# A gated attention and MLP decode step: one 128-row weight transfer cut into 102 and 26 rows

## The chip, the cores and the metric

The kernel runs on one core of a Trainium2 chip. The metric is the device time of one execution in microseconds (us), and the time of a kernel is the median of its runs. The profile used here records one execution: when each instruction of each engine ran, when each DMA packet moved, and when each DMA engine reported its share of a transfer done.

## The reference, cut to what matters

One token for each of 4 sequences passes through cached attention (32 heads of 128, a cache of 8192 positions) and through a gated MLP, and a sigmoid gate mixes the two.

```python
q = (x @ wq)                                  # [4, 32 heads, 1, 128]
p = softmax(einsum("bhqd,bhkd->bhqk", q, k_cache) * Dh ** -0.5)
o = einsum("bhqk,bhkd->bhqd", p, v_cache)     # [4, 32, 1, 128]
a = o.reshape(4, 1, 4096) @ wo                # wo: [4096, 1024]
y = ((silu(x @ w_gate) * (x @ w_up)) @ w_down) * sigmoid(x @ w_r)
b = x + y
g = sigmoid((x * gate_w).sum(-1))
return g * a + (1 - g) * b                    # [4, 1, 1024]
```

All inputs are bf16. The two caches are 268 MB each, and with the weights some 576 MB are read once.

## The kernel before

**A ring of SBUF and one queue.** All large inputs pass through one SBUF tile, `ring`, and every load into it is issued from SyncE's DMA queue in a hand-written order: wq, the gate, K and V of four heads at a time (`k_pair`, `v_pair`, 128 rows of 64 KB), w_up, w_down, the last V, and at the end wo. TensorE multiplies with the loaded data as the moving operand; VectorE turns K in 32x32 blocks.

**The tail.** wo is 4096 x 1024. `wov` views it as 8 blocks `g`, in each of which partition `p` holds 4 rows (slots `r` = 0 to 3, 2 KB each); a block is 1 MB. Blocks 0 and 1, and 2 and 3, come by one transfer each (`wo_two`); blocks 4, 5 and 6 by one each (`wo_block`, line 439). The last block, 7, comes in pieces so that TensorE can follow it closely: slots 0 and 1 in one transfer (512 KB), slot 2 in one (256 KB, 128 rows of 2 KB), and slot 3 in two halves of 512 columns (128 KB each, line 442). The list `cuts` holds these pieces:

```python
    cuts = [(g, 0, FR) for g in range(4, NWB - 1)] + [(NWB - 1, 0, 2), (NWB - 1, 2, 3)] + [(NWB - 1, FR - 1, FR, n) for n in range(NH)]
    last += [wo_block(*cut) for cut in cuts]
```

`wo_block` issues the load at once and returns `use`, which is called later and adds the block's products to two PSUM accumulators, `acc(0)` and `acc(1)`, one for each half of the 1024 output columns: per slot one matmul of 128 x 4 by 128 x 512 for each half (line 296, in `mm_acc`). The first half of slot 3 completes `acc(0)`, the second half completes `acc(1)`.

**The end.** VectorE copies `acc(0)` to SBUF (line 694) and SyncE's queue stores it (line 695); ScalarE copies `acc(1)` (line 696) and its own queue stores it (line 697).

**Semaphores of the transfers.** The transfers from SyncE take eight completion semaphores in turn. Before a transfer is issued on a semaphore, SyncE waits until the transfer that used it eight places earlier has landed, where nothing else implies that already.

**Engines of a transfer.** One transfer is divided by rows over DMA engines of the core (16 in all). Each engine works off its rows, one descriptor per row, then writes its completion (a packet of 4 bytes) and goes to its share of the next transfer in the queue. A transfer counts as landed when all of its engines have reported. Three early transfers are narrower than 128 rows: x (4 rows), two vectors of one row each, and, beside w_down, two transfers of 12 rows of 10 KB (line 411) and one of 8 rows of 2 KB (line 412).

Of the kernel before, what the change touches and what calls it, by code (L numbers as in the profile page):

```python
# [112 lines left out]
def kernel(  # L113
# [15 lines left out]
    nc = tc.nc  # L129
    P = 128  # L130
    Bn, Sq, D = A_x.shape
# [17 lines left out]
    FR = 4  # L149
    FG = F // (P * FR)  # L150
    NB = 512
    NH = D // NB
# [86 lines left out]
    n = 1  # L239
# [19 lines left out]
    for half in range(2):  # L259
        for e in range(2):  # L260
            nc.gpsimd.tensor_copy(out=R[:, 2 * half + e].rearrange("p (n j) -> p n j", n=4),
                                  in_=ident[:, 64 * half + e:64 * half + 64:2].unsqueeze(1).to_broadcast([P, 4, 32]))
# [21 lines left out]
    LT = const.tile([P, FR, H // FR, Bn], BF)  # L284
# [7 lines left out]
    def acc(n):  # L292
        return A_ps[n][32 * n:32 * n + Bn]

    def mm_acc(n, lhsT, rhs, start=False):
        nc.tensor.matmul(acc(n), lhsT=lhsT, rhs=rhs, start=start, stop=True, skip_group_check=True)  # L296
# [36 lines left out]
    wov = A_wo.rearrange("(g p r) n -> p g r n", p=P, r=FR)  # L333
# [86 lines left out]
    NWB = H // WB  # L420
# [8 lines left out]
                                 rhs=OT[:, WB * g0 + k:WB * g1:WB, :], start=True, stop=True, skip_group_check=True)  # L429
        nc.vector.tensor_copy(out=LT[:, :, g0:g1, :], in_=lp)  # L430

    def wo_block(g, r0=0, r1=FR, half=None, load=True):

        at = wo_places[g] * FR * D
        w = flat[:, at:at + FR * D].rearrange("p (r n) -> p r n", r=FR)
        if not load:
            pass
        elif half is None:
            nc.sync.dma_start(out=w[:, r0:r1].rearrange("p r n -> p (r n)"),
                              in_=wov[:, g, r0:r1].rearrange("p r n -> p (r n)"))  # L440
        else:
            nc.sync.dma_start(out=w[:, r0, half * NB:(half + 1) * NB], in_=wov[:, g, r0, half * NB:(half + 1) * NB])

        def use():
            for r in range(r0, r1):
                for n in range(NH) if half is None else [half]:
                    mm_acc(n, LT[:, r, g, :], w[:, r, n * NB:(n + 1) * NB])
        return use


    def wo_two(g):

        at = wo_places[g] * FR * D
        assert wo_places[g + 1] == wo_places[g] + 1
        nc.sync.dma_start(out=flat[:, at:at + 2 * FR * D].rearrange("p (g n) -> p g n", g=2),
                          in_=wov[:, g:g + 2].rearrange("p g r n -> p g (r n)"))
        return [wo_block(g, load=False), wo_block(g + 1, load=False)]
# [14 lines left out]
    def flush_sums():  # L472
        while full:
            full.pop(0)()
# [186 lines left out]
    for kind, d in order:  # L661
# [11 lines left out]
        if (kind, d) == ("v", ND - 1):  # L673
            first, second = wo_two(0)
            first()
            last = [second]
# [2 lines left out]
        if (kind, d) == ("v", ND - 2):  # L679
            o_rows(0, GE)  # L680
    last += wo_two(2)
    cuts = [(g, 0, FR) for g in range(4, NWB - 1)] + [(NWB - 1, 0, 2), (NWB - 1, 2, 3)] + [(NWB - 1, FR - 1, FR, n) for n in range(NH)]
    last += [wo_block(*cut) for cut in cuts]
    flush_sums()
    for _ in range(2):
        last.pop(0)()
# [41 lines left out]
```

## Time and profile before

| | us |
|---|---|
| median of 3 runs | 1341.02 |
| lowest, highest | 1340.89, 1341.03 |
| span of the profiled execution, first to last instruction | 1339.2 |
| last V transfer landed | 1321.01 |
| slot 2 of block 7 landed | 1335.32 |
| first half of slot 3 landed | 1335.66 |
| second half of slot 3 landed | 1335.98 |
| last matmul started | 1336.02 |

Times within the execution are from the start of its span. The median lies 1.8 us above the span of the profiled execution, which is the time around the span. "Landed" is the last of the transfer's engine reports in the trace.

### The profile page before, as it was taken

The page shows a single profiled execution, that of the slowest core. Times are in us where ns is not written, and L with a number is a line of the kernel's source. Part 1 is how long each engine was busy: PE and PEld are TensorE (multiplying, and loading weights), DVE is VectorE, ACT ScalarE, POOL GpSimd, SP SyncE. Part 2 cuts the span into 40 slices and gives each one's busy share as a digit, 9 for nine tenths or more (in the row PEclk, how much of TensorE's full clock was granted, in tenths as well). Part 3 has the DMA queues.
Part 4 walks back from the last instruction along what each step waited for, and adds up shares of the span by engine and source line. Part 5 has one row for each costly group of instructions (what it writes and reads, how often), then busy time and mean ns, then how long its engine had stood idle before and what let it go on. Part 6 is the DMA issues. An engine that isn't in the chain of part 4 may idle for free.

```text
span 1339.2 us, 6936 instructions
## 1 busy us (share of the span) xinstructions
PE 1031.3 (77%) x4654; PEld 139.8 (10%) x1486; DVE 638.7 (48%) x385; ACT 57.7 (4%) x58; POOL 67.0 (5%) x174
## 2 busy tenths in 40 slices
PE   2386787887777788777787977777797778687887
PEld 0011000001010010101001110100111011111111
DVE  2285998556553436555352556634345556100001
ACT  0000000100010000100010000100000000110000
POOL 2000000100010000100010000100001000100000
PEclk9697998898888998888889988888998889689999
DMA  9999999999999999999999999999999999999998
GB/s 415 433 437 437 435 437 435 420 438 433 433 435 437 427 433 435 429 438 431 433 431 433 435 439 427 429 433 435 438 430 428 433 429 429 438 429 445 422 422 352
DMA packets 13032, 576.14 MB, mean 430 GB/s; under 512 B 1436, under 2 KB 1700, under 8 KB 1970
## 3 DMA queue, kind: packets, MB, share of 16 engines
q1 hardware_dynamic: 12994, 575.69, 99.6%
q8 instruction: 24, 0.39, 0.1%
q14 instruction: 6, 0.05, 0.0%
q10 hardware_dynamic: 8, 0.00, 0.0%
HBM read 575.68 MB, written 0.01 MB: 430 GB/s over the span
## 4 chain that ended last, share of the span: by engine, by line
DMA 67%; PE 22%; DVE 9%; POOL 0%; ACT 0%; issue 0%; SPq 0%
DMA ring<-in_A_k_cache_dram 53%; PE S_ps L516 15%; DMA ring<-in_A_v_cache_dram 10%; DVE ring L511 9%; PE o_ps L587 5%; DMA ring<-in_B_w_gate_dram 3%; DMA ring<-in_A_wo_dram 2%; PE o_ps L342 1%; POOL PB L570 0%; DVE mx L536 0%; PE led L633 0%; ACT TB L545 0%; PE acc L296 0%; POOL Z L492 0%; PE o_ps L633 0%
## 5 line engine op out<-in xcount | busy, mean ns | idle before, releaser
L511 DVE STREAM_TRANSPOSE ring<-ring 128x2048 uint32<-128x2048 uint32 x256 | 566.5, 2276 | 307.7 <-DMA ring<-in_A_k_cache_dram 307.7
L516 PE MATMUL S_ps<-ring,Z 128*128 128x512 bf16 x2048 | 519.9, 408 | 229.3 <-DVE ring L511 216.1
L587 PE MATMUL o_ps<-ring,PB 128*64 128x512 bf16 x2048 | 457.4, 384 | 35.7 <-DMA ring<-in_A_v_cache_dram 33.3
L516 PEld LDWEIGHTS <-Z 128*128 128x128 bf16 x512 | 53.0, 104 | 683.0 <-issue 683.0
L617 DVE SCALAR_TENSOR_TENSOR OS<-o_ps,mE,OS 128x512 f32<-128x512 f32 x33 | 24.8, 751 | 161.7 <-ACT OS L613 160.2
L587 PEld LDWEIGHTS <-PB 128*64 128x64 bf16 x512 | 56.7, 111 | 428.3 <-issue 427.6
L625 DVE SCALAR_TENSOR_TENSOR OS<-o_ps,mE,OS 128x512 f32<-128x512 f32 x5 | 3.7, 750 | 143.6 <-ACT OS L623 143.6
L492 POOL COPY Z<-qa 32x4 bf16<-32x4 bf16 x128 | 25.8, 201 | 716.7 <-PE S_ps L516 689.6
L570 POOL COPY PB<-PT 32x1024 bf16<-32x1024 bf16 (+3 forms) x23 | 33.4, 1452 | 466.6 <-PE o_ps L587 360.7
L613 ACT ACTIVATE OS<-o_ps,mE 128x512 f32<-128x512 f32 x11 | 7.6, 687 | 671.2 <-PE o_ps L587 671.2
L568 ACT COPY PB<-PT 32x1024 bf16<-32x1024 bf16 (+3 forms) x21 | 30.3, 1444 | 22.4 <-PE o_ps L587 17.4
L545 ACT ACTIVATE TB<-S_ps,mx 128x2048 bf16<-128x2048 f32 x4 | 7.9, 1967 | 321.7 <-DVE mx L542 321.7
L254 PE MATMUL S_ps<-identb,x 6*128 6x6 bf16 x8 | 0.6, 196 | 22.3 <-DMA x<-in_gate_w_dram 22.3
L342 PE MATMUL o_ps<-ring,xw 128*4 128x512 bf16 (+2 forms) x128 | 12.9, 490 | 3.5 <-DMA ring<-in_B_w_gate_dram 3.5
L633 PEld LDWEIGHTS o_ps<-selg,OS 128*128 128x128 f32 x88 | 11.5, 191 | 8.8 <-issue 8.5
L550 DVE STREAM_TRANSPOSE PT<-TB 128x2048 bf16<-128x2048 bf16 x4 | 9.2, 2312 | 6.4 <-ACT TB L545 6.4
L296 PE MATMUL acc<-ring,hT 128*4 128x512 bf16 x54 | 7.9, 466 | 5.5 <-DMA ring<-in_B_w_down_dram 5.5
L536 DVE TENSOR_REDUCE mx<-S_ps 128x1 f32<-128x2048 f32 x4 | 9.1, 2282 | 6.0 <-PE S_ps L516 6.0
L296 PE MATMUL acc<-ring,LT 128*4 128x512 bf16 x64 | 8.8, 378 | 3.3 <-DMA ring<-in_A_wo_dram 2.8
L633 PE MATMUL o_ps<-selg,OS 128*128 128x8 f32 x88 | 10.5, 245 | 0.0
L623 ACT ACTIVATE OS<-o_ps,mE 128x512 f32<-128x512 f32 x5 | 3.4, 687 | 151.2 <-PE o_ps L587 151.2
L256 DVE COPY xw<-S_ps 128x48 bf16<-128x48 bf16 x1 | 0.2, 184 | 17.5 <-PE S_ps L254 17.5
(83 smaller groups left out, 88.4 us busy)
## 6 DMA issues: line engine op xcount, KB each, us to landing
ring<-in_A_v_cache_dram SPq DMA_DIRECT2D x7, 4096.0 KB
ring<-in_A_k_cache_dram SPq DMA_DIRECT2D x6, 4096.0 KB, 33.9
ring<-in_A_v_cache_dram SPq DMA_DIRECT2D x6, 2048.0 KB, 28.9
ring<-in_B_w_gate_dram SPq DMA_DIRECT2D x1, 7168.0 KB
ring<-in_B_w_up_dram SPq DMA_DIRECT2D x1, 7168.0 KB
ring<-in_B_w_down_dram SPq DMA_DIRECT2D x1, 6912.0 KB
ring<-in_A_wo_dram SPq DMA_DIRECT2D x2, 2048.0 KB
ring<-in_A_wo_dram SPq DMA_DIRECT2D x3, 1024.0 KB, 34.5
```

Source lines behind the costliest of these rows:

```text
L296: nc.tensor.matmul(acc(n), lhsT=lhsT, rhs=rhs, start=start, stop=True, skip_group_check=True)
L342: nc.tensor.matmul(ps[32 * k:32 * k + Bn, z, :].rearrange("p (f r) -> p f r", r=FR)[:, :, lo:hi], lhsT=xT[TW * half + t], rhs=rhs, start=( ...
L492: nc.gpsimd.tensor_copy(out=Z[at, :, QP - 1 + QP * q], in_=qa[at, :, h0 + q, b])
L511: nc.vector.transpose(out=kn[:, half], in_=kn[:, half])
L516: nc.tensor.matmul(sps[:, z, :], lhsT=Z[:, 2 * half + e, s:s + P], rhs=T[:, half, 16 * z:16 * z + 16, :, e], start=(t + k + half + e == 0) ...
L536: nc.vector.tensor_reduce(out=mx[:, 0:1], in_=sps[:].rearrange("p z n -> p (z n)"), axis=AX.X, op=ALU.max)
L550: nc.vector.transpose(out=PT[:].rearrange("p j i -> p (j i)"), in_=PTs)
L568: nc.scalar.copy(out=Bv[at, :, :, q, :], in_=Pv[at])
L570: nc.gpsimd.tensor_copy(out=Bv[at, :, :, q, :], in_=Pv[at])
L587: nc.tensor.matmul(o_ps[w // 2][row:row + NM, w % 2, :], lhsT=PB[:, RD * (d % NW) + n, z].rearrange("p w s j -> p (w s j)"), rhs=vn[:, j0 ...
L617: nc.vector.scalar_tensor_tensor(out=OS[:], in0=o_ps[w // 2][:, w % 2, :], scalar=mE[:, w:w + 1], in1=OS[:], op0=ALU.mult, op1=ALU.add)
L633: nc.tensor.matmul(oT, lhsT=OS[:, q * Dh:(q + 1) * Dh], rhs=selg[:, q].rearrange("p t s -> p (t s)"), start=(q == 0), stop=(q == 3), skip_ ...
```

## The change

Slot 2 of block 7 is loaded by two transfers, one of partitions 0 to 101 and one of partitions 102 to 127, in place of one transfer of 128 partitions. `wo_block` takes a column range in place of a half's number and a list of partition spans, and issues one transfer per span; all other pieces keep the one span of 128. The matmuls are the same in number, shape and order; they are written out in `use` in place of the call of `mm_acc`.

```diff
-    def wo_block(g, r0=0, r1=FR, half=None, load=True):
+    def wo_block(g, r0=0, r1=FR, cols=(0, D), load=True, spans=((0, P),)):
...
-        elif half is None:
-            nc.sync.dma_start(out=w[:, r0:r1].rearrange("p r n -> p (r n)"),
-                              in_=wov[:, g, r0:r1].rearrange("p r n -> p (r n)"))
-        else:
-            nc.sync.dma_start(out=w[:, r0, half * NB:(half + 1) * NB], in_=wov[:, g, r0, half * NB:(half + 1) * NB])
+        for p0, p1 in spans if load else ():
+            if c1 - c0 == D:
+                nc.sync.dma_start(out=w[p0:p1, r0:r1].rearrange("p r n -> p (r n)"),
+                                  in_=wov[p0:p1, g, r0:r1].rearrange("p r n -> p (r n)"))
+            else:
+                nc.sync.dma_start(out=w[p0:p1, r0:r1, c0:c1], in_=wov[p0:p1, g, r0:r1, c0:c1])
...
-                for n in range(NH) if half is None else [half]:
-                    mm_acc(n, LT[:, r, g, :], w[:, r, n * NB:(n + 1) * NB])
+                for n in range(NH):
+                    lo, hi = max(c0, n * NB), min(c1, (n + 1) * NB)
+                    if lo < hi:
+                        nc.tensor.matmul(acc(n)[:, lo - n * NB:hi - n * NB], lhsT=LT[:, r, g, :], rhs=w[:, r, lo:hi],
+                                         start=False, stop=True, skip_group_check=True)
...
-    cuts = [(g, 0, FR) for g in range(4, NWB - 1)] + [(NWB - 1, 0, 2), (NWB - 1, 2, 3)] + [(NWB - 1, FR - 1, FR, n) for n in range(NH)]
-    last += [wo_block(*cut) for cut in cuts]
+    cuts = [(g, 0, FR) for g in range(4, NWB - 1)] + [(NWB - 1, 0, 2), (NWB - 1, 2, 3)]
+    cuts += [(NWB - 1, FR - 1, FR, (n * NB, (n + 1) * NB)) for n in range(NH)]
+    last += [wo_block(*cut, spans=((0, 102), (102, P)) if cut[1:3] == (2, 3) and cut[0] == NWB - 1 else ((0, P),)) for cut in cuts]
```

More of the change, by code (lines that the diff above doesn't have):

```diff
@@ L430, in o_rows @@
         nc.vector.tensor_copy(out=LT[:, :, g0:g1, :], in_=lp)
-    def wo_block(g, r0=0, r1=FR, half=None, load=True):
+    def wo_block(g, r0=0, r1=FR, cols=(0, D), load=True, spans=((0, P),)):
         at = wo_places[g] * FR * D
+        c0, c1 = cols
         w = flat[:, at:at + FR * D].rearrange("p (r n) -> p r n", r=FR)
-        if not load:
-            pass
-        elif half is None:
-            nc.sync.dma_start(out=w[:, r0:r1].rearrange("p r n -> p (r n)"),
-                              in_=wov[:, g, r0:r1].rearrange("p r n -> p (r n)"))
-        else:
-            nc.sync.dma_start(out=w[:, r0, half * NB:(half + 1) * NB], in_=wov[:, g, r0, half * NB:(half + 1) * NB])
+        for p0, p1 in spans if load else ():
[4 more added lines that the diff above has]
+                nc.sync.dma_start(out=w[p0:p1, r0:r1, c0:c1], in_=wov[p0:p1, g, r0:r1, c0:c1])
         def use():
             for r in range(r0, r1):
-                for n in range(NH) if half is None else [half]:
-                    mm_acc(n, LT[:, r, g, :], w[:, r, n * NB:(n + 1) * NB])
+                for n in range(NH):
[3 more added lines that the diff above has]
+                                         start=False, stop=True, skip_group_check=True)
         return use
```

## The prediction, made before the changed kernel ran

> **What bounds the kernel now.** I read the page first, then the chain of waits of the last 40 us, then windows over the last 10 us, the timeline there, and SyncE's waits.
>
> ```profile
> span 1339.2 us, 6936 instructions
> ...
> DMA  9999999999999999999999999999999999999998
> ...
> q1 hardware_dynamic: 12994, 575.69, 99.6%
> q8 instruction: 24, 0.39, 0.1%
> ...
> DMA 67%; PE 22%; DVE 9%; POOL 0%; ACT 0%; issue 0%; SPq 0%
> ```
>
> The DMA engines are busy from start to end, and only the last slice of the span shows an 8. The kernel moves 576 MB, and the change moves not a byte less. What it can alter is the tail, so the tail's chain comes next (start, length, what):
>
> ```profile
> 1311.27 24.05 DMA ring<-in_A_wo_dram
> 1335.32 0.04 issue
> 1335.36 1.05 PE acc L296 x4
> 1336.41 0.02 issue
> 1336.43 0.58 ACT TB L696
> ```
>
> The end waits for wo: slot 2 of block 7 lands at 1335.32, four matmuls follow, then one copy and the store. The timeline and the windows (length, busy time of each engine, clock, DMA share, GB/s) show how:
>
> ```profile
> 1334.70 1.69 PE L296 MATMUL acc<-ring,LT 128*4 128x512 bf16 x8 [0.22 <-DMA ring<-in_A_wo_dram]
> 1336.12 0.68 DVE L694 CAST TB<-acc 4x512 bf16<-4x512 f32 x1 [6.49 <-PE acc L296]
> 1336.43 0.58 ACT L696 CAST TB<-acc 4x512 bf16<-4x512 f32 x1 [10.90 <-PE acc L296]
> ```
> ```profile
> 1328.00:1330.00 2.00, 2.00 (x35) 1.09 (x35) 0.43 (x2) 0.00 (x0) 0.00 (x0) 1.00 1.02 422
> 1331.00:1332.00 1.00, 1.00 (x8) 0.34 (x8) 0.00 (x0) 0.00 (x0) 0.00 (x0) 1.00 0.87 347
> 1332.00:1333.00 1.00, 0.02 (x2) 0.00 (x0) 0.00 (x0) 0.00 (x0) 0.00 (x0) 1.00 0.65 264
> 1334.00:1335.00 1.00, 0.78 (x10) 0.25 (x5) 0.00 (x0) 0.00 (x0) 0.00 (x0) 1.00 0.54 201
> ```
>
> The DMA share falls from 1.0 to 0.54 while work is still outstanding: engines run out of rows at different times. The trace's engine reports for the last transfer (second half of slot 3, all 16) say how different: four engines at 1331.23 to 1331.93, four at 1334.20 to 1334.76, eight at 1335.57 to 1335.98. The kernel waits for the last of these; the first is 4.75 us ahead. So the end is set by the slowest engine, not by the sum, and the question is which engines the two new transfers load.
>
> **Who is ahead, and why.** A 128-row transfer gives each engine 8 rows, and on each engine a packet starts as its predecessor ends (within some 4 ns), so the packets can be strung into 16 chains. Each of the 24 fetches of queue 8 (16 KB, about 1.1 us) breaks into one chain and puts it some 1.5 us behind. They take the same eight chains in turn, three rounds: 3 x 1.5 = 4.5 us, which is the gap between the first four and the last eight. The other eight chains take none of these fetches. At w_down, three of them carried the two 12-row transfers (2 x 4 rows of 10 KB, about 3.1 us): they are three of the middle four. The fourth of the middle was there before w_down.
>
> Which numbers have they? The narrow transfers reported 1, 1 and 4 engines for 1, 1 and 4 rows, 8 for 8 rows, 3 for the 12 rows (3 groups of 4 in memory), 16 for 128: always the largest number up to 16 that divides the outermost count of rows into equal shares. The three chains of the 12 rows also carry rows of the 8-row transfer, so narrow transfers start at the same first engine; call it 0. Engines 0 to 2 are then the three slowed ones. The 8-row transfer (0 to 7) also has two of the front chains, one of the middle group, and the first and second of the fetch order, but not the third. If the fetch order runs through neighbours, its first is 6, the second 7, the third 8, the eighth 13; untouched are 0 to 5, 14 and 15. That reading fits every narrow transfer; that 3, 4 and 5 are among the untouched is inferred, not shown.
>
> **The change part by part.** Rows first. By the rule of equal shares 102 rows go to 6 engines (17 each) and 26 to 13 (2 each). In place of 8 rows of 2 KB, engines 0 to 5 get 19, engines 6 to 12 get 2, engines 13 to 15 none. A 2 KB row takes 0.080 us in the chains (eight in 0.640 us), a completion 0.006. So:
> - engines 0 to 5: +11 rows and one completion more: 0.880 + 0.006 = +0.886 us;
> - engines 6 to 12: -6 x 0.080 = -0.480 us;
> - engines 13 to 15: -0.640 - 0.006 = -0.646 us.
>
> [...]
>
> Applied to the reports of the last transfer: the slowest of engines 0 to 5 goes from 1334.76 to 1335.65; the slowest of 6 to 12 from 1335.98 to 1335.50; 13 to 15 lie lower. The last landing becomes 1335.65, 0.33 us earlier. The same for the first half of slot 3: 1334.46 + 0.886 = 1335.35 (was 1335.66). For slot 2: its 26-row part on the same engine at 1334.11 + 0.89 = 1335.00 (was 1335.32).
>
> TensorE must keep up. Slots 0 and 1 land as before (1334.66); their four matmuls start at 1334.70 in pairs 0.21 us apart, so slot 2's pair can start at 1335.13 (was 1335.36). The first half follows at 1335.39, the second at 1335.69 (was 1336.02): each still waits for its data, so the gain passes whole. Copies and stores hang on these alone (lines 694 to 697) and move along.
>
> SyncE's queue. One transfer more shifts the two halves by one semaphore each.
>
> ```profile
> SPq L439 <- DMA ring<-in_A_v_cache_dram: 11.1, 3, 4.5
> SPq L442 <- DMA ring<-in_A_v_cache_dram: 9.0, 2, 4.5
> SPq L439 <- DMA ring<-in_A_wo_dram: 4.5, 1, 4.5
> ```
>
> SyncE sits waiting up to 4.5 us before each of these issues, for a transfer eight places back. The 102 rows go out at 1311.27 as the 128 did, the 26 rows at 1316.18, the first half at 1321.07 in place of 1316.18, and the second half waits for blocks 2 and 3 (landed 1325.98), going out near 1326.0 in place of 1321.07. From issue to first packet the output store took 0.76 us (1336.83 to 1337.59), so its rows are queued near 1326.9. The earliest engine reaches them near 1330.3, or 0.65 earlier if it is one that lost rows: some 2.8 us of cover, and about 8 us on the engines that end last. Without that cover, each us of late issue would count in full. Behind these issues in SyncE's queue stands only the output store, which waits for VectorE anyway. A narrow issue may take longer: the rows show 0.33 us for 128 rows, 0.44 for 8, 0.71 and 0.86 for 12; at most 0.5 us each, under 4.5 us of waiting: nothing. On TensorE one weight load of slot 2 takes a wait for the 26 rows beside the matmul's for the 102; a wait that is already met costs between nothing and the 0.04 us that the chain shows from landing to matmul, and slot 2 has 0.2 us of room before the first half: nothing.
>
> Unknown is whether a 17-row share runs at the pace of an 8-row one. Nearest row: the 12-row transfers' 10 KB rows took 0.385 to 0.396 us on 3 engines; the 8 KB row of full transfers (0.309) scaled to 10 KB is 0.386. So between nothing and 3% of 0.886, or 0.03 us; I take nothing, because most of those rows stand at the lower end.
>
> Sum: -0.33 us of landing, at most 0.03 back: -0.32. From the span 1339.2 to 1338.9, and from the median **1341.02 to 1340.7**. A measurement of this kernel can tell about 0.2% (2.7 us) from no change, so this counts as none.
>
> **The rivals.** *Engines 0 to 5 hold a late one* (slower). The fetch order need not run through neighbours; if any of 3, 4, 5 is one of the eight fetched chains, it gets +0.886 on 1335.57 to 1335.98. The time is then 1341.02 + 0.48 to 0.89, at most **1341.9**. It decides from the point where one of the six has less than 0.886 us of lead on the last. For it: only 0 to 2 are pinned by the 12-row transfers. Against it: the place of the first, second and third fetched chain about the 8-row transfer.
>
> *Fewer engines than six* (slower). Were 102 rows put on three, two or one engine, the slowest of these gets 34, 51 or 102 rows in place of 8, and up to 2 of the 26: +28, +45, +96 rows, or 2.2, 3.6, 7.7 us on 1334.76 at the latest. That ends 1.0, 2.4 or 6.5 us late: 1342.0, **1343.4** or 1347.5. For it: the 12 rows used only three engines. Against: those had an outermost 3 in memory, these rows have a plain 102.
>
> *Nothing changes.* Both transfers are spread over all 16 engines, the extra completion costs 0.006 us: **1341.0**. For it: 128-row transfers are spread so. Against: no narrow transfer here was. [...]
>
> **How the numbers follow.** Forecast 0.68, late engine among the six 0.14, nothing 0.12, fewer engines 0.06 (of which about half is over 2.7 us late, the two-engine case standing just under it). The forecast's own range: from -0.48, where engines 6 to 12 set the end, to -0.1 with the spread of the runs (0.14 us): 1340.5 to 1340.9. To hold 8 in 10 and the bounds of the unknowns I take in no change and the late engine: 1340.4 to 1341.9. Faster by over 0.2% no case gives: 0.01. Slower by over 0.2%: 0.03 of the fewer engines, and 0.01 for what I have not seen. Within: 0.95.
>
> **What would show it.** Right: six reports for the 102 rows and thirteen for the 26; the last transfer's reports closer together, the last at about 1335.65 on that clock; the DMA share of the last two us higher and ending sooner; the last matmul 0.3 us earlier against the last V. Wrong: a report of the last transfer later than 1335.98, a second half of slot 3 issued later than about 1329, or TensorE no longer waiting for DMA before the last matmul.

## The result, and the profile after

| | before | after |
|---|---|---|
| median | 1341.01 us (21 runs) | 1342.97 us (21 runs) |
| lowest to highest | 1340.80 to 1342.29 | 1342.57 to 1343.24 |
| profiled execution | span 1339.2 | time 1342.6, span 1340.8 |
| last V transfer landed | 1321.01 | 1321.13 |
| slots 0 and 1 of block 7 landed | 1334.66 | 1335.52 |
| slot 2 landed | 1335.32 | 1336.91 (26 rows; the 102 rows 1336.68) |
| first half of slot 3 landed | 1335.66 | 1337.20 |
| second half of slot 3 landed | 1335.98 | 1337.52 |

The ratio of after to before is 1.0013, with a 95% interval of 1.0007 to 1.0018. The kernel became 1.96 us slower. That is less than the 0.2% bound of the prediction, though the interval does not hold 1. The median is 1.1 us above the top of the forecast range (1341.9), and the sign is the other one. The profiled execution shows 1.6 us of it.

The page shows three packets more in queue 1 than before (12997 against 12994): the same rows, and 6 + 13 completions in place of 16.

```profile
span 1340.8 us, 6937 instructions
q1 hardware_dynamic: 12997, 575.69, 99.5%
```

The chain of waits of the last 40 us now runs through the 26 rows (start, length, what):

```profile
1289.13 27.11 DMA ring<-in_A_v_cache_dram
1316.24 0.02 issue
1316.26 20.65 DMA ring<-in_A_wo_dram
1336.91 0.04 issue
1336.95 1.00 PE acc L449 x4
1337.95 0.02 issue
1337.97 0.58 ACT TB L700
```

From the landing on, the chain is the same as before: 0.04 us, four matmuls in 1.00 us (1.05 before), one copy of 0.58 us. Everything lies 1.6 us later. The timeline says the same of TensorE: it waits for wo ahead of both last groups of matmuls.

```profile
1335.56 0.60 PE L449 MATMUL acc<-ring,LT 128*4 128x512 bf16 x4 [0.43 <-DMA ring<-in_A_wo_dram]
...
1336.95 0.99 PE L449 MATMUL acc<-ring,LT 128*4 128x512 bf16 x4 [0.80 <-DMA ring<-in_A_wo_dram]
```

SyncE's waits before the issues of the tail are those that the forecast laid out, one transfer later in the order (us in total, times, longest):

```profile
SPq L439 <- DMA ring<-in_A_v_cache_dram: 15.5, 4, 4.5
...
SPq L442 <- DMA ring<-in_A_wo_dram: 4.6, 1, 4.6
SPq L439 <- DMA ring<-in_A_wo_dram: 4.4, 1, 4.4
...
SPq L442 <- DMA ring<-in_A_v_cache_dram: 1.9, 1, 1.9
```

What did change is the rate of the DMA engines. These are windows of before and then of after (start, end and length, busy time of PE, PEld, DVE, ACT and POOL, granted clock, DMA share, GB/s):

```profile
1333.00:1334.00 1.00, 0.54 (x6) 0.26 (x7) 0.00 (x0) 0.00 (x0) 0.00 (x0) 1.00 0.74 276
1335.00:1336.00 1.00, 0.94 (x7) 0.17 (x4) 0.00 (x0) 0.00 (x0) 0.00 (x0) 1.00 0.16 54
```
```profile
1328.00:1330.00 2.00, 2.00 (x36) 1.21 (x36) 0.43 (x2) 0.00 (x0) 0.00 (x0) 1.00 1.01 414
1331.00:1332.00 1.00, 0.54 (x6) 0.26 (x7) 0.00 (x0) 0.00 (x0) 0.00 (x0) 1.00 0.82 287
1332.00:1333.00 1.00, 0.49 (x6) 0.09 (x1) 0.00 (x0) 0.00 (x0) 0.00 (x0) 1.00 0.78 281
1333.00:1334.00 1.00, 0.00 (x0) 0.00 (x0) 0.00 (x0) 0.00 (x0) 0.00 (x0) 1.00 0.73 229
1334.00:1335.00 1.00, 0.90 (x8) 0.34 (x8) 0.00 (x0) 0.00 (x0) 0.00 (x0) 1.00 0.75 261
1335.00:1336.00 1.00, 0.57 (x6) 0.09 (x3) 0.00 (x0) 0.00 (x0) 0.00 (x0) 1.00 0.49 141
```

Up to 1330 the two are near each other (414 against 422 GB/s, shown in the prediction). From 1331 to 1332 the rate is lower (287 against 347). After that GB/s alone cannot be compared, because more is left to move than before; GB/s divided by the DMA share can. In the window from 1333 to 1334 the engines are as busy as before (0.73 against 0.74), yet they move 229 GB/s in place of 276. Per fully busy set of engines that is 314 against 373, 16% less. The windows from 1331, 1332 and 1334 are lower in the same way (350, 360 and 348 against 399, 406 and 372). The work left over shows two us later: 141 GB/s where before only 54 were left to move.

The trace's packet records name the packets that got longer. From 1300 us on, an 8 KB row took at most 322 ns before and up to 496 ns after; a 2 KB row 85 ns in the mean and at most 95 before, 99 and up to 252 after. Most of the long packets lie where the 17-row shares of the 102 rows run, the first from about 1330.2 to 1331.9, the others from about 1332.7 to 1336.2. Not all do: some 8 KB rows that began between 1331.9 and 1332.3 took up to 474 ns.

The engine reports of the second half of slot 3 show one engine by itself: the last at 1337.52, the next at 1336.58. Strung into chains as in the prediction, this engine was one of the last eight before, and it is now one of the six with 17 rows. Its work ended 1.91 us later than before. Eleven rows and a completion more are 0.89 of that. Its packets also took 0.87 us longer than before at the same count: eight rows of 8 KB 2.68 us (2.47 before), eight of 4 KB 1.75 (1.25), its seventeen of 2 KB 1.53 (1.37 at 0.080 each). The remaining 0.15 is about the 0.12 by which the last V already landed late.

### The profile page after: what moved, and what is told of

Read it like the earlier page. It is cut to its first block, busy times and chain, and to the rows that moved or that the text cites. A ratio compares the mean times of both kernels' runs of the same rounds, so it can differ in the third digit from the quotient of the medians.

```text
span 1340.8 us, 6937 instructions
## 1 busy us (share of the span) xinstructions
PE 1033.6 (77%) x4654; PEld 140.7 (10%) x1486; DVE 638.8 (48%) x385; ACT 57.8 (4%) x58; POOL 66.6 (5%) x174
## 3 DMA queue, kind: packets, MB, share of 16 engines
q1 hardware_dynamic: 12997, 575.69, 99.5%
## 4 chain that ended last, share of the span: by engine, by line
DMA 68%; PE 21%; DVE 10%; ACT 0%; issue 0%; SPq 0%; DVEq 0%
DMA ring<-in_A_k_cache_dram 52%; PE S_ps L519 15%; DMA ring<-in_A_v_cache_dram 12%; DVE ring L514 10%; PE o_ps L590 5%; DMA ring<-in_B_w_gate_dram 3%; DMA ring<-in_A_wo_dram 2%; PE o_ps L342 1%; DVE OS L620 0%; DVE mx L539 0%; ACT TB L548 0%; PE acc L449 0%; ACT OS L616 0%; ACT TB L700 0%; SPq L228 0%
```

## The experiments

Two things thus seemed to add up, and three theories stood at the start of the runs. **A**: the number of rows. One of the six engines is among the last, and 11 rows more on it move the end by 0.89 us. **B**: the place of the rows. A share whose rows lie in partitions that other engines write in the 128-row transfers slows those engines and itself. **C**: the transfer by itself. One more transfer, or its slow issue (SyncE took 2.98 us to issue the 26 rows, 0.29 for the 102), costs the time. Each "before" below is the median of the runs on the same chip, and each landing is that of the last half of slot 3 in the profile (1335.98 before). Where a ratio's interval holds 1, the landings carry the reading, and each is that of one execution. In that execution the last V, which landed before any of the changed pieces did, can be late by itself: it landed at 1320.99 to 1321.47, against 1321.01 before. So the lateness counted from the last V stands in brackets behind each landing; the changed kernel's is 1.54 (1.42).

**112 and 16 partitions.** Both numbers divide by 16, so each engine gets 7 + 1 rows, as many as before; only where they lie changes.

```diff
-spans=((0, 102), (102, P))
+spans=((0, 112), (112, P))
```

> Slot 2 is cut into 112 and 16 rows in place of 102 and 26; both go to all 16 engines (7 rows and 1). Theory A (the loss is the 11 extra rows on an engine that is already among the last): every engine keeps 8 rows, so nothing moves, 1341.0 us. Theory B (engines slow each other when a share's rows lie in partitions that another engine writes in 128-row transfers): a share of 7 rows crosses such a border, 2 KB rows take over 84 ns, the end is 0.2 to 0.8 us later, 1341.2 to 1341.8. Theory C (a second transfer, or its slow issue of 2.98 us, costs by itself): as the changed kernel, near 1343.0.

Measured: 1342.21 us (11 runs) against 1341.13, ratio 1.0008 (0.9999 to 1.0017). Landing 1336.81, 0.83 late (0.68). Both transfers report 16 engines. 8 KB rows took up to 529 ns, 2 KB rows up to 227. No engine had a row more, so A gives nothing here, and B or C has to stand for it. The time lies between what B allowed at most (1341.8) and what C gave (1343.0).

**64 and 64 partitions, in blocks 4 to 6.** Slot 2 is whole again. Each of these three blocks arrives as two transfers of 64 partitions with 8 KB rows. By equal shares, as the reports show them for the other cuts (6 and 13 engines for 102 and 26 rows, 16 for 112 and for 16), every engine gets 4 + 4 rows.

```diff
-spans=((0, 102), (102, P)) if cut[1:3] == (2, 3) and cut[0] == NWB - 1 else ((0, P),)
+spans=((0, 64), (64, P)) if cut[0] in (4, 5, 6) else ((0, P),)
```

> Blocks 4, 5 and 6 (1 MB each) are loaded as two transfers of 64 rows each; slot 2 of block 7 is whole. All transfers go to 16 engines (4 rows and 4). Theory A: no engine gets more rows, 1341.0. Theory B: if an engine's share is 4 neighbouring rows, 16 engines write into 64 partitions at a time that 8 engines write in 128-row transfers; 8 KB rows take up to twice the 309 ns, over 3 MB (7.3 us at full pace) up to 7 us more: 1343 to 1348. Theory C: three more transfers at some tenths of a us each, 1341.5 to 1343.

Measured: 1352.39 us (4 runs) against 1341.13, ratio 1.0084 (1.0070 to 1.0098). Landing 1346.16, 10.2 late (9.9). The 8 KB rows of the three blocks took 575 ns in the median, against 313 before. The loss is more than the 7 us that B allowed at most; the pieces behind the blocks were slow too (4 KB rows 237 ns in the mean, 164 before). TensorE's granted clock was 0.50 from 1331 to 1336 and 0.62 from 1344 to 1348, and TensorE too was late at the end, so part of the last us is its own; the packet times do not hang on that.

**The same reads, to even and to odd partitions.** As the run above, but the first 64 rows in memory go to the 64 even partitions, the last 64 to the odd ones. The rows of wo in blocks 4 to 6 meet other rows of the product than they should; the work is the same.

```diff
+to = w[p0:p1] if p1 - p0 == P else w[p0 // 64:P:2]
-nc.sync.dma_start(out=w[p0:p1, r0:r1].rearrange("p r n -> p (r n)"),
+nc.sync.dma_start(out=to[:, r0:r1].rearrange("p r n -> p (r n)"),
```

> As the 64 and 64 run, but the first 64 rows of memory go to the even partitions and the last 64 to the odd ones (the products of blocks 4 to 6 so pair rows of wo with other rows of the attention output). The reads are the same as in that run; only the place in SBUF differs. Theory B (slowing at the partitions written): the 16 engines write to all 128 partitions again, so most of the loss of the 64 and 64 run is gone, 1341.0 to 1342.5. If the slowing is on the side of the reads from memory, the time equals that of the 64 and 64 run. Theory A: 1341.0 in both.

Measured: 1341.33 us (10 runs) against 1341.13, ratio 1.0001 (0.9992 to 1.0010). Landing 1336.08, 0.10 late (0.04 early). 8 KB rows 313 ns, at most 326. The same transfers in the same order, with the same bytes from the same addresses, differ by 11 us in time and 10 us in landing through the partitions that they write. The windows of the kernel before, of the neighbouring partitions, and of even and odd ones show the DMA engines wholly busy at 424, 229 and 418 GB/s:

```profile
1322.00:1326.00 4.00, 3.62 (x21) 0.57 (x11) 1.01 (x2) 1.27 (x2) 0.00 (x0) 1.00 1.02 424
```
```profile
1322.00:1326.00 4.00, 3.90 (x22) 0.65 (x12) 0.73 (x2) 1.26 (x2) 0.00 (x0) 1.00 1.00 229
```
```profile
1322.00:1326.00 4.00, 3.77 (x21) 0.57 (x11) 0.87 (x2) 1.26 (x2) 0.00 (x0) 1.00 1.00 418
```

B stands, and three more transfers cost nothing that can be measured: C has lost most of its ground.

**68 and 60 partitions.** By equal shares 68 rows go to 4 engines (17 each), 60 to 15 (4 each). Engines 0 to 3 then get 21 rows in place of 8, all others 4 or none.

```diff
-spans=((0, 102), (102, P))
+spans=((0, 68), (68, P))
```

> Slot 2 is cut into 68 and 60 rows: 4 engines with 17 rows, 15 with 4. Engines 0 to 3 get 21 rows (+13, +1.05 us), 4 to 14 get 4 (-0.32 us), 15 none. Theory A: if engine 3 is not the late one, the last landing is max(1334.76 + 1.05, 1335.98 - 0.32) = 1335.81, 0.17 us early, 1340.8; if engine 3 is the late one, 1342.1. Theory B: 17-row shares slow the others as well, another 0.3 to 0.6 us later, 1341.1 to 1341.6. Theory C: 1343.0.

Measured: 1341.95 us (11 runs) against 1341.13, ratio 1.0007 (0.9998 to 1.0016). Landing 1336.76, 0.78 late (0.60). The 68 rows report on four engines, at 1334.62, 1334.75, 1334.79 and 1335.75: engines of the middle group, with no late one among them. 8 KB rows took up to 493 ns. The 13 extra rows alone would have brought the slowest of the four to 1335.81, ahead of the 1335.98 of the kernel before. The end is later through the slowing, and by more than B allowed (1341.6).

**Six extra rows, each on an engine of its own.** To part A from B, five runs took the kernel before and added one transfer behind slot 2, of 6 or fewer rows of 22 KB (22,528 bytes; the expectations say 22.5 KB) from the V cache into a part of the ring that is no longer used. A row is 11 x 2 KB, so each of its engines gets the bytes that the 11 rows of 2 KB had. What is varied is the distance of the rows' partitions.

```diff
+            if (g, r0) == (NWB - 1, 2):
+                nc.sync.dma_start(out=flat[0:48:8, 12 * FR * D:12 * FR * D + 11 * D], in_=kv_view(A_v_cache, 0)[0:6, 0:11 * D])
```

> Slot 2 is whole; behind it one more transfer of 6 rows (22.5 KB each, of the V cache, to a part of the ring that is no longer read) loads engines 0 to 5 with one row each, 0.83 us at their pace, to partitions 0, 8, ... 40. No other engine gets or loses a row. Theory A (one of engines 0 to 5 is among the last eight): its last report goes from 1335.57 to 1335.98 up by 0.84, 1341.5 to 1341.9; if none of the six is, 1341.0, for 1334.76 + 0.84 = 1335.60 lies before 1335.98. Theory B (engines slow each other at the partitions written): if an engine's own partitions are 8 neighbours, each of these rows takes its 0.83 us and nothing else slows; if they are fours, rows take up to twice that, and 1342 to 1343.

In the next run the partitions are four apart:

```diff
-flat[0:48:8, ...]
+flat[0:24:4, ...]
```

> The same six rows to partitions 0, 4, ... 20. Theory A as with partitions 8 apart. Theory B the other way round: 0.83 us per row and nothing slowed if an engine's own partitions come in fours, up to 1.7 us per row, 1342 to 1343, if they are 8 neighbours.

And in the third they are neighbours:

```diff
-flat[0:48:8, ...]
+flat[0:6, ...]
```

> The same six rows to partitions 0 to 5, side by side. Theory A alone: as the other two, 1341.5 to 1341.9. Theory B: all six engines write to the partitions of one or two; if these take together what one engine moves (27 GB/s), the 135 KB need 5.0 us, rows of several us are seen, and the end is 2 to 4 us late, 1343 to 1345.

| partitions of the six rows | median (10 runs) / before (31 runs) | ratio | landing | the six packets, us |
|---|---|---|---|---|
| four apart | 1341.74 / 1341.21 | 1.0003 (0.9994 to 1.0013) | 1336.82, +0.84 (+0.38) | 0.836 to 0.871 |
| eight apart | 1342.34 / 1341.21 | 1.0006 (0.9997 to 1.0015) | 1337.30, +1.32 (+1.33) | 0.860 to 1.182 |
| neighbours | 1342.97 / 1341.21 | 1.0012 (1.0002 to 1.0021) | 1337.74, +1.76 (+1.50) | 1.102 to 2.201 |

Four apart is the clean case: no other packet became longer (8 KB rows at most 324 ns). That its landing is late by just the 0.84 us of one packet is chance. The last V was already 0.46 late, and 0.38 is left. This fits one packet on a late engine that is not the last: strung into chains, that engine is the first of the eight late ones. It reported at about 1335.6 before, 0.37 ahead of the last, and 0.84 less 0.37 is 0.47. Eight apart has the same bytes on the same number of engines and costs 0.48 us of landing more (0.95 counted from the last V), with 8 KB rows up to 631 ns. The windows of the two, four apart first, show it at the same DMA share:

```profile
1333.00:1334.00 1.00, 0.08 (x2) 0.08 (x3) 0.00 (x0) 0.00 (x0) 0.00 (x0) 1.00 0.77 307
```
```profile
1333.00:1334.00 1.00, 0.53 (x6) 0.26 (x7) 0.00 (x0) 0.00 (x0) 0.00 (x0) 1.00 0.78 251
```

Neighbours slow each other as well, though by less than the 2 to 4 us expected; that the six did not start at the same time is a likely reason, not a shown one. In the run four apart the chain ends in the two matmuls of a late half, behind the landing of the first half at 1336.50 (1335.66 before):

```profile
1321.48 15.02 DMA ring<-in_A_wo_dram
1336.50 0.04 issue
1336.55 0.71 PE acc L296 x2
```

**Which of the six is late?** The same with four and with five rows, four partitions apart, beside the kernel before (1340.97, 19 runs).

```diff
-flat[0:24:4, ...], kv_view(A_v_cache, 0)[0:6, ...]
+flat[0:16:4, ...], kv_view(A_v_cache, 0)[0:4, ...]
```

> As the run with six rows 4 partitions apart (its last landing was 0.84 us late and no packet was slowed), but with four rows, on engines 0 to 3. If the late engine among the six is 4 or 5: the four are engines of the middle group, 1334.76 + 0.84 = 1335.60 lies before 1335.98, nothing changes, 1341.0, last half at 1336.0. If it is one of 0 to 3: last half again near 1336.8, 1341.8.

```diff
-flat[0:24:4, ...], kv_view(A_v_cache, 0)[0:6, ...]
+flat[0:20:4, ...], kv_view(A_v_cache, 0)[0:5, ...]
```

> Five rows, on engines 0 to 4. If engine 4 is the late one, as with six rows: last half near 1336.8, 1341.8; if it is 5, as with four: 1336.0 and 1341.0.

| rows | median, ratio | landing | reports of the extra transfer |
|---|---|---|---|
| four | 1341.05, 1.0001 (0.9991 to 1.0010) | 1335.94 (-0.02) | 1334.20, 1334.33, 1334.49, 1335.04 |
| five | 1341.17, 1.0000 (0.9991 to 1.0010) | 1336.15 (+0.10) | 1331.98, 1334.51, 1334.56, 1334.57, 1335.10 |
| six (above) | 1341.74, 1.0003 (0.9994 to 1.0013) | 1336.82 (+0.38) | 1332.44, 1334.76, 1334.85, 1335.01, 1335.50, 1336.16 |

The fifth row adds a report that is early, the sixth one that is late. So engines 0 to 3 are the middle group, 4 is one of the first four, and 5 is one of the last eight. The six reports of the 102 rows in the changed kernel have the same pattern: 1332.64, four from 1334.71 to 1335.76, and 1336.68. Up to five rows the end is set elsewhere, as the chain of the run with five shows: it has the four matmuls of slot 2 onward and the 1.06 us of the kernel before.

```profile
1335.48 0.04 issue
1335.52 1.06 PE acc L296 x4
```

Both runs have one narrow transfer more than the kernel before, and cost nothing that can be measured. With 112 and 16 partitions SyncE took 0.33 and 0.31 us for the two issues, and the loss was there all the same. C has fallen.

**102 and 26 partitions on the first half of slot 3.** The same cut on a piece with 1 KB rows, slot 2 whole. Eleven rows are half as long there.

```diff
-if cut[1:3] == (2, 3) and cut[0] == NWB - 1 else ((0, P),)
+if cut[3:] == ((0, NB),) else ((0, P),)
```

> Slot 2 is whole, and the first half of slot 3 (1 KB rows, 0.042 us each) is cut into 102 and 26 instead. Engines 0 to 5 get 11 rows of 1 KB more, 0.47 us in place of 0.886. Theory A: a late engine among the six ends 0.47 us later than before at most, 1341.1 to 1341.5. Theory B: half the foreign bytes, half the slowing of the changed kernel (0.87 us), another 0.4: 1341.5 to 1341.9.

Measured: 1341.81 us (10 runs) against 1341.21, ratio 1.0004 (0.9995 to 1.0014). Landing 1336.68, 0.70 late (0.60); 8 KB rows up to 406 ns. The same cut costs less where the rows are shorter, and more than the 0.47 us that A gives at most, which fits A and B together. It is the cut that costs, and not slot 2.

## Why the prediction was wrong

**What held.** The end is set by the slowest DMA engine (its report at 1337.52, the next at 1336.58), and TensorE waits for it up to the last matmul (started at 1337.56). The shares are 6 and 13 engines. SyncE issued the 102 rows at 1311.41, the 26 at 1316.26 and the halves at 1321.20 and 1326.17; the forecast had 1311.27, 1316.18, 1321.07 and 1326.0, and no engine ran out of rows before the second half came. The price of 11 rows, 0.886 us, is also right where nothing slows them: a packet of the same bytes took 0.836 to 0.871 us in the run with six rows four apart. The rivals "fewer engines than six" and "nothing changes" fall with the six and thirteen reports and the later landing.

**The first step that failed: the numbering.** The prediction said of engines 0 to 5 "that 3, 4 and 5 are among the untouched is inferred, not shown". For 3 and 4 that holds. Engine 5 is one of the eight that the fetches of queue 8 put behind; the run with six rows against the run with five shows it. The fetch order does not run from 6 through 13, as the prediction took it to. This was the rival "engines 0 to 5 hold a late one", at 0.14, and it priced what it named rightly: +0.886 on a report in the last group. Alone it would have ended at 1341.9 at most.

**The second: "whether a 17-row share runs at the pace of an 8-row one".** I bounded that term between nothing and 0.03 us and took nothing. On the engine that ended last, its own rows and the 8 and 4 KB rows near them took 0.87 us longer. Only 0.16 of this is the pace of the 17 rows, the term that was named. The other 0.71 lies in the rows of whole 128-row transfers ahead of them, and for these the sum had no term. The row it was sized from, 10 KB rows of the 12-row transfers at 0.385 to 0.396 us, came from 3 engines at w_down: it had neither 17 partitions in one share nor six such shares at a time, so it showed nothing of the cost that mattered. The 112 and 16 and the 68 and 60 runs have this slowing without a row more on a late engine, 0.83 and 0.78 us of landing (0.68 and 0.60 counted from the last V).

The landing adds up so: forecast 1335.65, measured 1337.52, 1.87 late. Of this 0.87 is the slowing. The engine reported at about 1335.6 before; 0.886 more is 1336.5, which is 0.84 above the forecast, and the 0.15 left over on this engine makes it 1.0. Neither alone would have left the range: the rows alone end 0.5 us later than the 1335.98 of the kernel before, and the other engines, slowed as well, had reported by 1336.58, 0.6 later. The two on the same engine leave it.

The slowing is shown as far as this: with the same reads, the time follows from the partitions written (575 ns an 8 KB row to 64 neighbours, 313 to 64 even or odd ones; the 575 ns are 1.84 times the 313), and single rows are clean four partitions apart (0.836 to 0.871 us, 8 KB rows at most 324 ns) but not eight (0.860 to 1.182 us, 8 KB rows up to 631 ns). What in the hardware makes writes to some partitions slow each other, no run shows.

For the cut itself the runs show that it costs between nothing that can be measured (even and odd partitions, 1341.33 us against 1341.13) and 11 us (neighbouring ones, 1352.39), by the partitions that it writes.

**Open.** Which rows of a transfer each engine takes was not measured, so why even and odd partitions are without any loss is not shown. Nor is whether some cut could win: none of the runs beat the kernel before, and rows that are moved off a late engine are written by others, which by theory B can slow both. Why the 26 rows took 2.98 us to issue, where the forecast allowed 0.5 us more, is not known. It does not follow from their number alone: 26 rows of 1 KB took 0.60 us in the run on the half, and a whole 128-row transfer took 2.55 us in the kernel before (block 4, at 1291.85). It cost nothing here, since SyncE still waited 1.9 us before the next issue.

## What to carry to other kernels

Cutting a full 128-partition load by partitions changed two things here that the byte count does not show: how many rows each engine carries (17 of the 102 on each of 6 engines, 2 of the 26 on each of 13, in place of 8 on each of 16), and which partitions are written at the same time (229 GB/s against 418 with the same reads). When the end hangs on the slowest DMA engine, find out which engine is late before giving it more, by adding one row at a time, here four partitions apart, and reading where its report falls (the fifth row's at 1331.98, the sixth's at 1336.16). And when a term is sized from a nearest row, ask whether that row has the cost in question at all; this one could not have shown it.

## What the runs showed of the hardware

- Transfers cut into two of 64 neighbouring partitions each ran at little more than half the rate: 229 GB/s against 418 with even and odd partitions and 424 with whole 128-partition transfers, with the DMA share at 1.00 to 1.02 in all three.
- Slowed DMA engines counted as busy. The DMA share from 1333 to 1334 was 0.73 and 0.78 with 229 and 251 GB/s in two slowed runs (102 and 26 rows, six rows eight apart), and 0.74 and 0.77 with 276 and 307 GB/s in two others (the kernel before, six rows four apart); only the GB/s and the packet times show the loss.
- The eight engines that the 24 fetches put behind are not 6 to 13: by the six, five and four rows 5 is one of them, and 0 to 4 are not.
- SyncE took 2.98 us to issue the transfer of 26 rows of 2 KB, and 0.29 us for that of 102; whole 128-row transfers took 0.33 us, and one of them 2.55.
